# Order of the last value products, a zeroed warm-up matrix and an earlier cast of x in a gated attention and feed-forward kernel

## The chip, the cores and the metric

The kernel runs on one core of one Trainium2 chip. The metric is the device time of one execution in microseconds; several executions are timed, and their median counts. A further execution was profiled, and the profile is of that one.

## The reference, cut to what matters

The input x has 2048 rows of 512. A sigmoid gate g per row mixes two branches: a causal attention of 32 heads of 16 columns over a sliding window of 256 rows, and a feed-forward block with a SiLU gate and 1792 hidden columns.

```python
qkv = (x @ wqkv).reshape(B, S, 3, H, Dh)          # S=2048, D=512, H=32, Dh=16, W=256
scores = einsum("bhqd,bhkd->bhqk", q, k) * Dh ** -0.5
mask = (idx[:, None] - idx[None, :] >= 0) & (idx[:, None] - idx[None, :] < W)
p = softmax(where(mask, scores, -1e9))
a = einsum("bhqk,bhkd->bhqd", p, v) ... @ wo
b = (silu(x @ w_gate) * (x @ w_up)) @ w_down
g = sigmoid((x * gate_w).sum(-1))
out = g * a + (1 - g) * b
```

## The kernel before

**Tiling.** x is kept transposed, in four chunks of 512 columns (c = 0 to 3), each in four pieces of 128 rows. Precision is kept by splitting operands in two: `split` (L63) casts a high part on ScalarE (`xhi`) and subtracts it from the source on another engine (`xlo`); a projection then takes three products for each piece: high by high, low by high and high by low (`products`, L113; `whole`, L191, records at L195). The 32 heads are worked in 8 groups of 4. All order is written out by hand: each engine carries out its instructions in program order, and a tile that is needed before it is ready stops the engine that needs it.

**The start.** SyncE's queue fetches the first weights and x's first chunk piece by piece, alternating (L430 to L432), then the value weights and x's other three chunks (L433 to L436). In the meantime TensorE multiplies an identity, made by GpSimd (`make_identity`, L45), five times with itself into a tile that nobody reads (L173 to L175). Such a float32 product is two matmul instructions with a weight load each. Then come the first projections from the raw pieces (two groups, L444, 16 matmuls), value products (`vproj`) and projections of groups 0 and 1 over the later chunks, in the order of L461 to L475. `split_x(c)` (L426) is what makes a chunk of x ready: four casts on ScalarE, four subtractions on VectorE. `split_x(3)` stands at L471, behind `run(proj(1, 1, ...))` (L470), whose last act is a copy out of PSUM on ScalarE, a cast there, and a subtraction on GpSimd. The loop at L474 then projects group 0 over chunks 2 and 3.

**The main loop.** For each group and block of 128 rows (L628), scores are computed twice: `stage1` (L263) for the row maxima of the next group, `stage2` (L305) transposed for the exponentials of this one, which ScalarE writes (L307) and GpSimd masks (L309, L312). Between them TensorE works off projections and feed-forward products in two row halves (`lanes`, L215).

**The value products.** `av(g, c)` (L317) multiplies the exponentials by the values for a chunk of 512 queries. Blocks of 128 keys are named by their place m relative to the chunk's start, −2 to 3; block m touches only the queries within its window, so products near the chunk's edges are narrow. The lower 64 keys of a block go through the first 64 rows of the array into one PSUM tile, the other 64 through the last 64 rows into another tile, so two products run side by side, for each of four heads in its own 32 columns: eight products a step. L323 gives each half its own order of blocks, such that both products of a step have the same width:

| step | half 0 | half 1 | columns |
|---|---|---|---|
| 1 | m = 0 | m = 0 | 320 |
| 2 | 1 | 1 | 320 |
| 3 | 2 | −1 | 256 |
| 4 | −1 | 2 | 192 |
| 5 | −2 | 3 | 64 |
| 6 | 3 | −2 | 128 |

Chunk 0 has no blocks before it: negative m drop out there, and four steps are left, with m = 0, 1, 2, 3 in both halves. `values(t)` (L612) calls `av` three times a group: for chunks 0 and 1 together, for chunk 2 and for chunk 3. Behind each call the loop goes on with `stage1` and `stage2`. `finish` (L334) adds the two tiles, beginning with a copy on ScalarE (L342), and divides by the sums.

**The end.** Behind the main loop come the feed-forward block's last products and the output projection (L736, L83 to L85).

Of the kernel before, what the change touches and what calls it, by code (L numbers as in the profile page):

```python
# [8 lines left out]

F32 = mybir.dt.float32  # L10
F32R = mybir.dt.float32r
# [5 lines left out]
P = 128  # L17
# [16 lines left out]
def gated_mix(ctx, tc, xT, xn, w01, wqk, wv, wo, wgu, wd, gw, out):  # L34
# [4 lines left out]
    nc = tc.nc  # L39
    ctx.enter_context(tc.manual_schedule())  # L40

    const = ctx.enter_context(tc.tile_pool(name="const", bufs=1))
    dram = ctx.enter_context(tc.tile_pool(name="dram", bufs=1, space=DRAM))

    ident = const.tile([P, P], F32, name="ident")  # L45
    make_identity(nc, ident)
    vd = dram.tile([G, P, NB, VW], F32, name="vd")
    od = dram.tile([G, P, S], F32, name="od")
    mxd = dram.tile([2 * G, P, 32], F32, name="mxd")
# [13 lines left out]
    def split(hi, lo, src, hi_eng, lo_eng):  # L63
        if hi_eng is nc.scalar:
            nc.scalar.copy(hi, src)
        else:
            hi_eng.tensor_copy(hi, src)
        lo_eng.tensor_tensor(out=lo, in0=src, in1=hi.bitcast(F32), op=ALU.subtract)

    def fetch(src, raw=None):  # L70

        raw = ring.tile([P, D], F32, name="raw", bufs=1) if raw is None else raw
        nc.sync.dma_start(raw, src)
        return raw
# [14 lines left out]
    def run(gen, n=None):  # L89

        while n is None or n > 0:
            if next(gen, run) is run:
                break
            n = n and n - 1
# [5 lines left out]
    def slot(name, dtype=F32R):  # L100
        return stk.tile([P, S], dtype, name=name)

    def halves_of(t):
        n = t.shape[-1] // 2
        return [t[:, :n], t[:, n:]]
# [7 lines left out]
    def products(key, c):  # L113
        wh, wl = WT[key]
        return [(wt[:, k], xt[c][:, k]) for k in range(NK) for wt, xt in ((wh, xhi), (wh, xlo), (wl, xhi))]
# [53 lines left out]
    with ExitStack() as A:  # L169
# [1 line left out]


        warm = pp.tile([P, CH], F32, name="pa")  # L173
        for _ in range(5):
            nc.tensor.matmul(warm[:, :P], ident, ident, start=True, stop=True)  # L175

        mask = sm.tile([P, 3 * P], F32, name="mask", bufs=1)

        def kept():
            return sm.tile([P, CH], F32, name="ev", bufs=EV)  # L180
# [3 lines left out]
        def x_pair(pool=None, name="x"):  # L184
            return tuple((pool or sm).tile([P, 2 * CH], F32R, name=f"{name}{w}", bufs=1) for w in ("hi", "lo"))

        def split_qk(g, hf, cc, raw, los=nc.gpsimd):
            hi, lo = (t[:, cc * CH:(cc + 1) * CH] for t in X[g, hf])
            split(hi, lo, raw, nc.scalar, los)

        def whole(pool, name, todo, done):  # L191

            ps = pool.tile([P, CH], F32, name=name)
            for n, (w, x) in enumerate(todo):
                nc.tensor.matmul(ps, w, x, start=n == 0, stop=n == len(todo) - 1)  # L195
                if n < len(todo) - 1:
                    yield
            done(ps)
            yield
# [30 lines left out]
        def proj(g, c, pool, name, todo=None, los=nc.gpsimd):  # L230

            hf, cc = divmod(c, 2)
            if cc == 0:
                X[g, hf] = x_pair() if g == hf else x_pair(vpool, f"x{g}{hf}")

            def done(ps):
                raw = kept()
                nc.scalar.copy(raw, ps)
                split_qk(g, hf, cc, raw, los)
            return whole(pool, name, todo or products(("p", g), c), done)  # L240

        def stack(g, hf):
            for pr in range(2):
                q, k = (halves_of(t[g % 2][pr])[hf] for t in (QT, KT))
                hi, lo = (x[32 * pr:] for x in X[g, hf])
                for b, (qx, kx) in enumerate(((hi, hi), (hi, lo), (lo, hi))):
                    nc.sync.dma_start(q[b::4].bitcast(F32), qx[:32].bitcast(F32))
                    nc.sync.dma_start(k[b::4].bitcast(F32), kx[64:96].bitcast(F32))
# [68 lines left out]
        def av(g, c):  # L317


            AV[g, c] = (pp.tile([P, CH], F32, name="pb" if 4 * g + c + 1 < len(UNITS) else "pa"),  # L320
                        ps2.tile([P, CH], F32, name="ps2"))

            orders = [[4 * c + m for m in ms if 4 * c + m >= 0] for ms in ((0, 1, 2, -1, -2, 3), (0, 1, -1, 2, 3, -2))]  # L323
            for n, kbs in enumerate(zip(*orders)):
                for j in range(4):
                    for h, (o, kb) in enumerate(zip(HALVES, kbs)):
                        k0 = kb * P + 64 * h
                        q0, q1 = max(k0, c * CH), min(k0 + W + 64, c * CH + CH)
                        nc.tensor.matmul(AV[g, c][h][32 * j:32 * j + 32, q0 - c * CH:q1 - c * CH],  # L329
                                         VG[4 * g + kb // 4][o, kb % 4, 17 * j:17 * j + 32],  # L330
                                         PT[g, kb, j // 2][o, j % 2, q0 - kb * P:q1 - kb * P],
                                         start=n == 0, stop=n == len(orders[0]) - 1, skip_group_check=True)
# [61 lines left out]
        def v_products(b):  # L394
            c, o = divmod(b * P, CH)
            return [(xt[c][:, k, o:o + P], wt[:, k]) for k in range(NK)
                    for xt, wt in ((xhi, wvh), (xlo, wvh))] + \
                   [(xhi[c][:, k, o:o + P], wvl[:, k]) for k in range(NK)]
# [6 lines left out]
        def put_v(b, ps):  # L405
            t = vs[b // 2 % 2]
            nc.scalar.copy(t[:, :, b % 2, :68].rearrange("p g (j e) -> p g j e", e=17)[:, :, :, :DH],
                           ps.rearrange("p (g j e) -> p g j e", j=4, e=DH))
            if b > 3:
                send_v(b)  # L410

        def vproj(b):
            return whole(pp, "pb", v_products(b), lambda ps: put_v(b, ps))
# [8 lines left out]
        xraw = [h for w in "qk" for pr in range(2) for h in halves_of(slot(f"{w}1{pr}", F32))]  # L422
        xraw = [halves_of(h) for h in xraw]
        xraw = [[xraw[2 * c + k // 2][k % 2] for k in range(NK)] for c in range(NCH)]

        def split_x(c, ks=range(NK)):  # L426
            for k in ks:
                split(xhi[c][:, k], xlo[c][:, k], xraw[c][k], nc.scalar, nc.vector)

        for k in range(NK):  # L430
            nc.sync.dma_start(w01raw[:, k], w01[k])
            nc.sync.dma_start(xraw[0][k], xT[0, k])  # L432
        wvraw = [fetch(wv[:, k], kept()) for k in range(NK)]  # L433
        for c in range(1, NCH):
            for k in range(NK):
# [31 lines left out]
        run(proj(0, 1, pp, "pa", los=nc.vector))  # L467
        stack(0, 0)
        run(vproj(3))
        run(proj(1, 1, pp, "pa"))  # L470
        split_x(3)  # L471
        QT.append([slot(f"q1{pr}") for pr in range(2)])
        KT.append([slot(f"k1{pr}") for pr in range(2)])
        for c in range(2, NCH):  # L474
# [137 lines left out]
        def values(t):  # L612

            ag, m = divmod(t - 8, NB)
            if m == 0:
                cs, times = (0, 1), [((0, 1),) * 2 + ((0, 3), (2, 0), (2, 3)), ((0, 1), (0, 2), (1, 1), (3, 2), (4, 1))]
            else:
                cs, times = (1 + m // 4,), [((0, 1), (0, 2), (1, 1), (2, 1), (3, 1))]
            for c in cs:
                av(ag, c)  # L620
            for k, steps in enumerate(zip(*(finish(ag, c) for c in cs))):
                for todo, ts in zip(steps, times):
                    dt, hd = ts[k]
                    if (dt, hd) == (0, 1):
                        todo()
                    else:
                        FIN.setdefault((t + dt, hd), []).append(todo)
        for t in range(G * NB + 1):  # L628
# [26 lines left out]
            m = (t - 3) % NB + 3  # L655
# [188 lines left out]
```

## Time and profile before

| | us |
|---|---|
| median of 3 runs | 820.35 |
| lowest and highest | 819.96 and 820.63 |
| the profiled execution | 819.19 |
| its span in the profile | 817.2 |

In the profile PE is TensorE's matmuls, PEld its weight loads, DVE VectorE, ACT ScalarE, POOL GpSimd, SPq SyncE's queue. A row of a timeline has the start and the duration in us, the engine, the line, the operation, the tiles (out<-in), the size and the count; in square brackets stands how long the engine was idle ahead of it and who ended that. PE is busy for 810.5 us (99%), but ends of matmuls are modelled, and several overlap; DVE is busy for 63% of the span, ACT for 55%, POOL for 42%. The granted TensorE clock of the profiled execution is 1.0.

### The profile page before, as it was taken

How to read it: one execution, taken by the hardware profiler on the slowest of the kernel's cores; microseconds unless marked ns; L12 is line 12 of the kernel's file. 1: busy time of each engine (PE TensorE's matmuls, PEld its weight loads, DVE VectorE, ACT ScalarE, POOL GpSimd, SP SyncE). 2: the span in 40 equal slices, each digit the busy share in tenths (PEclk: the TensorE clock that was granted, in tenths of full speed). 3: DMA queues.
4: the chain of work that ended last, by engine and by line, in shares of the span. 5: the costliest groups of instructions: out<-in, count | busy, mean ns of one | idle time of the engine just before them, and what ended most of it. 6: DMA issues, size and time to landing. Idle time of an engine off the chain costs nothing.

```text
span 817.2 us, 21557 instructions
## 1 busy us (share of the span) xinstructions
PE 810.5 (99%) x8306; PEld 681.7 (83%) x8306; DVE 513.5 (63%) x1422; ACT 452.9 (55%) x940; POOL 343.4 (42%) x635
## 2 busy tenths in 40 slices
PE   9999999999999999999999999999999999999997
PEld 5788988888888888898888888888788888888886
DVE  5596667667668667677677678854467443443542
ACT  6422656656666666676666665666666423343341
POOL 5812546645546555654554654465610111011020
PEclk9999999999999999999999999999999999999999
DMA  8484615625634642652652565565689444463731
GB/s 295 113 262 145 182 68 165 195 76 151 184 109 118 189 147 85 175 174 70 187 179 89 161 185 165 161 217 171 216 302 322 156 139 141 159 203 103 221 89 52
DMA packets 70326, 133.27 MB, mean 163 GB/s; under 512 B 14288, under 2 KB 19024, under 8 KB 70224
## 3 DMA queue, kind: packets, MB, share of 16 engines
q1 hardware_dynamic: 65936, 116.95, 46.3%
q0 software_dynamic: 4288, 14.95, 5.1%
q8 instruction: 65, 1.06, 0.6%
q14 instruction: 37, 0.30, 0.1%
HBM read 61.08 MB, written 45.61 MB: 131 GB/s over the span
## 4 chain that ended last, share of the span: by engine, by line
PE 95%; DMA 2%; POOL 1%; SPq 1%; DVE 0%; issue 0%; ACT 0%; ACTq 0%
PE pb L215 24%; PE pa L215 24%; PE ps L85 6%; PE ps L83 6%; PE ps L84 6%; PE ps L263 6%; PE pb L329 6%; PE ps L305 5%; PE ps L329 3%; PE pb L85 2%; PE pb L83 2%; PE pb L84 2%; PE pa L736 1%; PE pb L736 1%; PE pb L195 1%; DMA k<-xT 1%
## 5 line engine op out<-in xcount | busy, mean ns | idle before, releaser
L265 DVE CUSTOM_DVE_ANT_0 ps<-ps,mask 128x384 f32<-128x384 f32 (+2 forms) x512 | 273.1, 540 | 119.0 <-PE ps L263 68.7
L307 ACT ACTIVATE pt<-ps 128x384 f32<-128x384 f32 (+2 forms) x512 | 239.4, 476 | 117.9 <-PE ps L305 57.5
L309 POOL TENSOR_SCALAR_AFFINE_SELECT pt<-pt 128x256 f32<-128x256 f32 x256 | 109.1, 426 | 222.3 <-ACT pt L307 209.3
L305 PE MATMUL ps<-q,k 64*128 64x384 f32 (+2 forms) x512 | 159.7, 326 | 0.0
L263 PE MATMUL ps<-k,q 63*128 63x384 f32 (+2 forms) x512 | 157.9, 328 | 0.0
L215 PE MATMUL pb<-xhi,wh 64*128 64x512 f32 x512 | 110.9, 393 | 0.0
L215 PE MATMUL pa<-xhi,wh 64*128 64x512 f32 x512 | 110.7, 393 | 0.0
L215 PE MATMUL pb<-xhi,wl 64*128 64x512 f32 x512 | 109.8, 392 | 0.0
L215 PE MATMUL pb<-xlo,wh 64*128 64x512 f32 x512 | 109.8, 391 | 0.0
L215 PE MATMUL pa<-xlo,wh 64*128 64x512 f32 x512 | 109.3, 391 | 0.0
L215 PE MATMUL pa<-xhi,wl 64*128 64x512 f32 x512 | 109.1, 391 | 0.0
L263 PEld LDWEIGHTS ps<-k,q 63*128 63x128 f32 x512 | 88.8, 185 | 14.2 <-issue 4.0
L312 POOL TENSOR_SCALAR_AFFINE_SELECT pt<-pt 128x256 f32<-128x256 f32 x224 | 96.9, 433 | 0.0
L305 PEld LDWEIGHTS ps<-q,k 64*128 64x128 f32 x512 | 91.4, 185 | 5.9 <-issue 0.6
L329 PE MATMUL ps<-pt,vg 64*32 64x320 f32 (+4 forms) x1408 | 75.1, 346 | 0.0
L740 DVE TENSOR_TENSOR sg<-got,sg 128x512 f32<-128x512 f32 x50 | 43.7, 874 | 48.1 <-ACT sg L739 48.1
L329 PE MATMUL pb<-pt,vg 64*32 64x320 f32 (+3 forms) x1360 | 72.3, 350 | 0.1
L265 DVE DVE_READ_ACCUMULATOR2_ANT mx<- 128x1 f32 x512 | 72.2, 141 | 0.0
L329 PEld LDWEIGHTS pb<-pt,vg 64*32 64x32 f32 x1360 | 48.8, 106 | 20.8 <-ACT pt L307 5.8
L215 PEld LDWEIGHTS pb<-xhi,wh 64*128 64x128 f32 x512 | 55.8, 185 | 8.1 <-ACT ev L529 0.2
L215 PEld LDWEIGHTS pa<-xhi,wh 64*128 64x128 f32 x512 | 55.7, 185 | 7.5 <-ACT ev L529 0.6
L215 PEld LDWEIGHTS pb<-xhi,wl 64*128 64x128 f32 x512 | 55.8, 184 | 7.1
(163 smaller groups left out, 1555.6 us busy)
## 6 DMA issues: line engine op xcount, KB each, us to landing
raws<-ev SPq DMA_DIRECT2D x100, 256.0 KB
got<-raws SPq DMA_DIRECT2D x100, 256.0 KB
od<-on POOLq DMA_DIRECT2D x32, 256.0 KB, 2.6
raw<-wgu SPq DMA_DIRECT2D x28, 256.0 KB
q<-xhi SPq DMA_DIRECT2D x56, 128.0 KB
k<-xhi SPq DMA_DIRECT2D x56, 128.0 KB
vd<-vs POOLq DMA_DIRECT2D x8, 672.0 KB, 6.0
vg<-vd SPq DMA_DIRECT2D x32, 168.0 KB
```

What stands on the lines that cost most here:

```text
L83: nc.tensor.matmul(ps, lh, rh, start=start and i == 0, stop=False)
L84: nc.tensor.matmul(ps, lh, rl, start=False, stop=False)
L85: nc.tensor.matmul(ps, ll, rh, start=False, stop=stop and i == n - 1)
L215: mm = nc.tensor.matmul(ps[me], w[r], x[r], start=not second and i == 0, stop=bool(second) and i == n - 1)
L263: nc.tensor.matmul(ps[:, :n], QT[g % 2][pr][r, q0:q0 + P], KT[g % 2][pr][r, k0:k0 + n], start=True, stop=True)
L265: mx = nc.vector.tensor_tensor_reduce(out=ps[:, :n], in0=ps[:, :n], in1=mask[:, 3 * P - n:], scale=1.0, scalar=NEG, op0=ALU.add, op1=ALU.m ...
L305: nc.tensor.matmul(ps[:, :n], KT[g % 2][pr][r, k0:k0 + P], QT[g % 2][pr][r, k0:k0 + n], start=True, stop=True)
L307: BEHIND.append(nc.scalar.activation(pt[:, j, :n], ps[:, :n], AF.Exp, scale=SCALE))
L309: nc.gpsimd.affine_select(out=pt[:, :, :P], in_=pt[:, :, :P], pattern=[[0, 2], [1, P]], compare_op=ALU.is_ge, fill=0.0, base=0, channel_mu ...
L312: nc.gpsimd.affine_select(out=pt[:, :, 2 * P:], in_=pt[:, :, 2 * P:], pattern=[[0, 2], [-1, P]], compare_op=ALU.is_ge, fill=0.0, base=-1, ...
L329: nc.tensor.matmul(AV[g, c][h][32 * j:32 * j + 32, q0 - c * CH:q1 - c * CH], VG[4 * g + kb // 4][o, kb % 4, 17 * j:17 * j + 32], PT[g, kb, ...
L740: nc.vector.tensor_tensor(out=sg, in0=gu[1], in1=sg, op=ALU.mult)
```

## The change

Three places are edited.

- In `av` the last two steps of the six change places: the products of 128 columns come fifth, those of 64 columns sixth, in both halves. For chunk 0 the lists stay as they are.
- The warm-up matrix is a tile of zeros, written by one VectorE memset at the head of that engine's work; GpSimd makes no identity any more. The warm-up has six products instead of five. The first piece of x is fetched by ScalarE's queue; all other loads stay on SyncE's.
- `split_x(3)` stands ahead of `run(proj(1, 1, ...))` instead of behind it.

```diff
-from concourse.masks import make_identity
...
-    ident = const.tile([P, P], F32, name="ident")
-    make_identity(nc, ident)
+    zero = const.tile([P, P], F32, name="zero")
+    nc.vector.memset(zero, 0.0)
...
-        for _ in range(5):
-            nc.tensor.matmul(warm[:, :P], ident, ident, start=True, stop=True)
+        for _ in range(6):
+            nc.tensor.matmul(warm[:, :P], zero, zero, start=True, stop=True)
...
-            orders = [[4 * c + m for m in ms if 4 * c + m >= 0] for ms in ((0, 1, 2, -1, -2, 3), (0, 1, -1, 2, 3, -2))]
+            orders = [[4 * c + m for m in ms if 4 * c + m >= 0] for ms in ((0, 1, 2, -1, 3, -2), (0, 1, -1, 2, -2, 3))]
...
             nc.sync.dma_start(w01raw[:, k], w01[k])
-            nc.sync.dma_start(xraw[0][k], xT[0, k])
+            (nc.sync if k else nc.scalar).dma_start(xraw[0][k], xT[0, k])
...
         run(vproj(3))
+        split_x(3)
         run(proj(1, 1, pp, "pa"))
-        split_x(3)
```

## The prediction

> **What bounds the kernel now.** I read the page first: the chain that ended last is matmul time on TensorE for nearly the whole span, so a nanosecond taken off TensorE's own sequence is a nanosecond off the end, and DVE, ACT and POOL matter only where TensorE waits for one of them.
>
> ```profile
> span 817.2 us, 21557 instructions
> ...
> PE 95%; DMA 2%; POOL 1%; SPq 1%; DVE 0%; issue 0%; ACT 0%; ACTq 0%
> ```
>
> Second I read the waits of the weight loads (PEld) over the whole span: who was waited for, us in total, times, longest.
>
> ```profile
> PEld ps L263 <- issue: 4.0, 20, 0.2
> ...
> PEld ps L305 <- issue: 0.6, 3, 0.2
> ...
> PEld pa L736 <- issue: 0.2, 1, 0.2
> ```
>
> These are 20 + 3 + 1 = 24 waits of 0.2 us, 4.8 us in all, and nothing is waited for. Twenty-four is also the number of places where the value products (L329) end: 8 groups with three runs each (chunks 0 and 1 together, then 2, then 3). So third I read the timeline of one such place, first TensorE's matmuls (start us, us).
>
> ```profile
> 128.85 0.32 PE L329 MATMUL pb<-pt,vg 64*32 64x192 f32 x1
> ...
> 129.02 0.22 PE L329 MATMUL pb<-pt,vg 64*32 64x64 f32 x1
> ...
> 129.13 0.27 PE L329 MATMUL pb<-pt,vg 64*32 64x128 f32 x1
> ...
> 129.44 0.27 PE L329 MATMUL ps<-pt,vg 64*32 64x128 f32 x1
> 129.64 0.44 PE L263 MATMUL ps<-k,q 63*128 63x384 f32 x1
> ```
>
> Eight products (four heads by two row halves) run side by side, each in two passes. The eight 64-column products have both passes started and streamed between 129.02 and 129.13: 0.056 us a pass. Then come the 128-column ones. The first starts at once, at 129.13; the last starts its second pass only at 129.44. Streaming alone would put that at 129.13 + 0.11 + 0.05 = 129.29. Why it is late stands in the weight loads of the same stretch:
>
> ```profile
> 129.07 0.16 PEld L329 LDWEIGHTS pb<-pt,vg 64*32 64x32 f32 x2
> 129.21 0.10 PEld L329 LDWEIGHTS ps<-pt,vg 64*32 64x32 f32 x1
> ...
> 129.34 0.11 PEld L329 LDWEIGHTS ps<-pt,vg 64*32 64x32 f32 x1
> 129.64 0.18 PEld L263 LDWEIGHTS ps<-k,q 63*128 63x128 f32 x1 [0.20 <-issue]
> ```
>
> The load for the second 128-column product goes out only at 129.21, and the rest are strung out until 129.34, when the last product begins its first pass (the load for a product's second pass goes out as its first begins). From there to the next line's load is 129.64 − 129.34 = 0.30 us: two passes of 0.107 (129.34 to 129.44 is one) and 0.09 to empty the array, behind which the 128-wide load of L263 goes.
>
> What holds the load at 129.21? It is 0.04 behind the recorded end (128.85 + 0.32 = 129.17) of the second pass of a 192-column product, which stands 17 products earlier in the program. I read this as a window of some 16 products: the next is let in when an old one is done. [...]
>
> **The swap (L323).** In chunks 1 to 3 the last two of the six steps change places: 128 columns, then 64. Nothing is added or removed, and chunk 0 keeps its order, since steps at negative blocks drop out. The 192-column products that open the window stay where they are, so the loads of the last step's products go out when they do now, and the last product begins its first pass at about 129.34 again, now with 64 columns. The 128-column step ahead of it starts at 129.02 and has streamed its two passes by 129.02 + 2 × 0.107 + 0.05 = 129.28, so it is not later than that. What is left behind the last load is two passes of 0.056 in place of two of 0.107: 0.10 us saved, with the 0.09 to empty the array unchanged. Times 24: 2.4 us. Bounds: if the next load went a fixed 0.20 behind the start of the last pass, whatever its length, only one pass is shortened, 0.05 × 24 = 1.2 us. If nothing held the loads, the last first pass would start 0.05 sooner (129.28 + 0.01), 0.15 × 24 = 3.6 us. I take 2.4, because 0.20 splits well into a pass of 0.107 and a remainder, and because the loads have a visible cause that does not move. What follows the place on TensorE is again bound by TensorE, by the chain. ACT's copy of the sums is released 0.10 sooner, and nothing waits for it there. The data of the newest block is first needed in the fifth step in both orders, so no new wait.
>
> [...]
>
> **x's last quarter cast sooner (L471 to before L470).** Fourth I looked at the one other place where TensorE waits visibly:
>
> ```profile
> 28.70 0.59 ACT L238 COPY ev<-pa 128x512 f32<-128x512 f32 x1 [2.12 <-PE pa L195]
> ...
> 29.84 2.18 ACT L65 CAST xhi<-k 128x512 fp32r<-128x512 f32 x4
> ...
> 30.49 1.98 DVE L68 TENSOR_TENSOR xlo<-k,xhi 128x512 fp32r<-128x512 f32 x2 [3.68 <-DMA k<-xlo]
> ...
> 30.99 0.39 PE L195 MATMUL pa<-xhi,wl 128*128 128x512 f32 x1
> ...
> 31.22 0.39 PE L195 MATMUL pa<-xhi,wh 128*128 128x512 f32 x1
> ...
> 31.91 0.19 PEld L195 LDWEIGHTS pa<-xlo,wh 128*128 128x128 f32 x1 [0.73 <-DVE xlo L68]
> 31.92 0.50 PE L195 MATMUL pa<-xlo,wh 128*128 128x512 f32 x1 [0.31 <-DVE xlo L68]
> ```
>
> The projection over x's last quarter has its second matmul at 31.92 instead of 31.22 + 0.23 = 31.45: 0.47 us lost, and a little at the restart (0.50 against 0.39 for that matmul), so 0.6. It waits for DVE's first subtraction, that for ACT's first cast at 29.84 (DVE's wait is named as a DMA, but the cast ends as it ends), and ACT stands idle for 2.12 us before 28.70, in program order behind a copy that waits for TensorE. The moved step is four casts and four subtractions, no DMA. In that gap, from 28.70 − 2.12 = 26.58, the casts take 2.18 and end at 28.76. The copy they now stand ahead of slips by 0.06, and with it the cast and the POOL subtraction behind it; they feed a stack that is sent long after. DVE was idle for 3.68 us in the same stretch and has the first subtraction done near 28, over 3 us ahead of need. All 0.6 goes, if x's last quarter has landed by 26.58. A bound for that: the load issued behind it in the same queue had landed at
>
> ```profile
> 15.15 5.14 DMA raw<-wgu
> ```
>
> 15.15 + 5.14 = 20.29. What is late next is TensorE itself. Bounds: 0.47 and 0.6; I take 0.6.
>
> **The head.** The warm-up reads a zeroed matrix, made by one DVE memset, in place of POOL's memset and select, and has six products (12 matmuls) instead of five; x's first piece goes out from ACT's queue at once rather than second on SP's.
>
> ```profile
> 1.26 0.42 SPq L432 DMA_DIRECT2D q<-xT  x1
> 1.32 1.22 POOL L388 MEMSET vs<- 128x1344 f32 x1
> 1.43 2.21 PEld L175 LDWEIGHTS pa<-ident 128*128 128x128 f32 x10 [1.43 <-POOL ident masks.py:199]
> ...
> 4.17 7.51 PE L195 MATMUL pa<-q,vs 128*128 128x512 f32 x16 [0.23 <-DMA q<-xT]
> ```
>
> SP's 14 later loads go out 0.45 sooner (0.42 of issuing and a gap), x's first piece likewise. But the warm-up now holds TensorE for 2.21 / 10 × 12 = 2.65 us, 0.44 more, from perhaps 0.1 sooner (the memset is short and first on DVE): to about 4.0 or 4.1, where the products of x begin at 4.17 today. So they begin 0.1 sooner. No price on ACT: its table load waits for one DMA issue and has over a microsecond to spare before x is there. POOL only loses work. How much of an earlier start survives ACT's casts behind it no row shows; bounds are one issue spacing either way, 0.45 sooner or 0.45 later (two queues sharing the engines may bring the first weights or a later piece later). I take 0.1, nearest to where the longer warm-up ends.
>
> **Sum.** 2.4 + 0.6 + 0.1 = 3.1 us. The profiled execution took 819.19 us (span 817.2), 1.2 below the median of 820.35. The sum makes it 816.1, and the median 820.35 − 3.1 = 817.25; I say 817.3.
>
> **Rivals.** All keep 0.6 + 0.1 unless said.
> - *Fixed delay*: the next line's load follows the last pass's start by 0.20 whatever its length. 1.2 + 0.7 = 1.9: 818.5. For it: all 24 waits are 0.2. Against it: all 24 end on the same width, so they can't tell, and 0.09 after a pass is a more natural emptying.
> [...]
> - *The zeroed matrix does not wake the clock.* Of the 16 matmuls from 4.17 on one took 1077 ns, the others 592 (min, median, max):
>
> ```profile
> L195 PE MATMUL pa<-q,vs x16: 592/592/1077, 4.2 to 11.1; 128*128 128x512 f32 x16
> ```
>
> I read this as full speed from about 5.1, 3.7 us after the warm-up began. With a warm-up that counts for nothing it would come 3.7 after 4.1, 2.7 later than now, and half-speed work over that time costs 1.3: 820.35 − 3.1 + 1.3 = 818.6. Against it: the identity is itself all zeros but for one element a row, and it seems to have been enough.
> - *Slower*: the hold in the loads is not set 17 products back but by the step's own first product, 129.21 − 129.13 = 0.08 behind it, and a 64-column pass can't cover the 0.107 of its own load. Then after the swap: first product at 129.24, last load 129.24 + 0.08 + 0.09 (the loads' spread now) = 129.41, first pass 0.03 later, second pass 0.107 later (129.55), and the next load 0.20 behind: 129.75 against 129.64, 0.11 × 24 = 2.6 lost, less 0.7: 822.2. It decides as soon as the hold exceeds what the shorter passes give, 0.10. Against it: the 64-column loads now come ahead of their own step's first product.
>
> **How the numbers follow.** The forecast has 0.62 (with it the better end, 816.0 or so), the fixed delay 0.15, no gain from the swap 0.11, the clock 0.07, slower 0.05. The range holds the forecast with its bounds (2.4 to 3.6, and 0.45 at the head: down to 820.35 − 3.6 − 0.6 − 0.45 = 815.7), the fixed delay, the clock and no gain from the swap: 815.7 to 819.7. About 0.2%, 1.6 us, is what a measurement of this kernel can tell from no change: up to 818.7 counts as faster. That is the forecast but for its worst end, two thirds of the fixed delay, half of the clock: 0.74. Same is the rest without the slower case: 0.21.
>
> **What would show it.** In the profile after: the 24 waits named issue still there, but the last L329 matmul 64 columns wide, and from the first 192-column pass at such a place to the next load of L263 0.10 us less, with the loads of the last step starting where they start now. PEld's wait on xlo gone, ACT's idle 2.12 filled by the four casts, the copy of L238 at 28.7 to 28.8 (less what the head gives). The products of x starting at 4.0 to 4.1. Wrong would be: last loads moved by more than 0.05, the next load again 0.20 behind the last pass's start, a second matmul of x at over 0.43 us spacing for long (clock), or the first wait for a DVE or ACT row in the run of matmuls from 34 us on.

## The result and the profile after

| | before | after |
|---|---|---|
| median (6 runs each) | 820.49 | 816.29 |
| lowest to highest | 819.8 to 821.34 | 815.41 to 816.6 |
| the profiled execution | 819.19 | 815.41 |
| its span | 817.2 | 813.7 |

After to before 0.9947, 95% interval 0.9934 to 0.996: 4.2 us less (3.3 to 5.4 by the interval's ends), where 3.1 were forecast. The two profiled spans differ by 3.5. Lines of the kernel after are one lower, since an import is gone: its L328 is L329 before.

The weight loads' waits of after, whole span, as shown of before:

```profile
PEld pb L194 <- issue: 0.8, 3, 0.3
...
PEld ps L262 <- issue: 0.2, 1, 0.2
```

Of the 24 waits of 0.2 us at the ends of the value products one is left in the list, which shows none of 0.15 us or less; the others have become shorter (0.09 at most places). The wait on x's low part is gone from the list. The same place as before, TensorE's matmuls first:

```profile
127.49 0.32 PE L328 MATMUL pb<-pt,vg 64*32 64x192 f32 x1
...
127.66 0.27 PE L328 MATMUL pb<-pt,vg 64*32 64x128 f32 x1
...
127.77 0.27 PE L328 MATMUL pb<-pt,vg 64*32 64x128 f32 x1
...
127.87 0.22 PE L328 MATMUL pb<-pt,vg 64*32 64x64 f32 x1
...
128.03 0.22 PE L328 MATMUL ps<-pt,vg 64*32 64x64 f32 x1
128.17 0.44 PE L262 MATMUL ps<-k,q 63*128 63x384 f32 x1
```

and its weight loads:

```profile
127.77 0.11 PEld L328 LDWEIGHTS pb<-pt,vg 64*32 64x32 f32 x1
127.85 0.10 PEld L328 LDWEIGHTS ps<-pt,vg 64*32 64x32 f32 x1
...
127.97 0.11 PEld L328 LDWEIGHTS ps<-pt,vg 64*32 64x32 f32 x1
128.17 0.18 PEld L262 LDWEIGHTS ps<-k,q 63*128 63x128 f32 x1
```

The 128-column step now starts both its passes on the beat (127.66, 127.77). The hold in the loads is still there: the second load of the last step goes out at 127.85, 0.36 behind the point at which the second passes of the 192-column step begin (127.49), and before it was 129.21 − 128.85 = 0.36 as well. The last load is at 0.48 behind that point (127.97), before at 0.49. From it to the next line's load are 0.20 us now (128.17) and 0.30 before. That is the gain of 0.107, and it stands at 17 of the 24 places in the trace (0.105 to 0.108).

At six places, those where a new group's first scores follow, it is smaller: 0.05 at five, 0.02 at one. There the last value product is followed by this:

```profile
L262 PEldq EVENT_SEMAPHORE  x3: 51/51/51, 144.1 to 144.3; - x3
L262 PEld LDWEIGHTS ps<-k,q x1: 183/183/183, 144.4 to 144.4; 63*128 63x128 f32 x1
```

Three instructions in TensorE's own queue that only wait for semaphores start 0.11 us apart, and the load behind them is what now ends last. At one place the gain is 0.24: before, its last step was held up for 0.13 us, by what no row shows (POOL's last mask ahead of it had ended 2.9 us earlier). In sum 2.3 us over the 24 places.

x's last quarter, timelines of after (ACT, DVE and PE rows):

```profile
25.82 2.18 ACT L64 CAST xhi<-k 128x512 fp32r<-128x512 f32 x4
...
26.48 2.50 DVE L67 TENSOR_TENSOR xlo<-k,xhi 128x512 fp32r<-128x512 f32 x4 [0.48 <-ACT xhi L64]
...
28.06 0.59 ACT L237 COPY ev<-pa 128x512 f32<-128x512 f32 x1
...
30.58 0.39 PE L194 MATMUL pa<-xhi,wh 128*128 128x512 f32 x1
30.81 0.39 PE L194 MATMUL pa<-xlo,wh 128*128 128x512 f32 x1
```

The second product follows the first by 0.23 where it was 0.70. And the start:

```profile
1.12 2.93 PE L174 MATMUL pa<-zero 128*128 128x128 f32 x12 [1.12 <-DVE zero L45]
4.22 7.27 PE L194 MATMUL pa<-q,vs 128*128 128x512 f32 x16 [0.17 <-DMA q<-xT]
```

The first product of x is not earlier (4.22, before 4.17), but the 16 matmuls take 7.27 instead of 7.51, and the first projection over x's second chunk began at 19.70 instead of 20.34.

### The profile page after: what moved, and what is told of

Same layout as the page of the kernel before. It is cut to its first block, busy times and chain, and to the rows that moved or that the text cites. A ratio compares the mean times of both kernels' runs of the same rounds, so it can differ in the third digit from the quotient of the medians.

```text
span 813.7 us, 21560 instructions
## 1 busy us (share of the span) xinstructions
PE 807.6 (99%) x8308; PEld 697.7 (86%) x8308; DVE 512.2 (63%) x1423; ACT 453.6 (56%) x940; POOL 343.1 (42%) x633
## 4 chain that ended last, share of the span: by engine, by line
PE 99%; DMA 0%; ACT 0%; DVE 0%; issue 0%; ACTq 0%
PE pb L214 24%; PE pa L214 24%; PE ps L83 6%; PE ps L82 6%; PE ps L84 6%; PE ps L262 6%; PE pb L328 6%; PE ps L304 5%; PE ps L328 3%; PE pa L194 2%; PE pb L194 2%; PE pb L83 2%; PE pb L82 2%; PE pb L84 2%; PE pa L735 1%; PE pb L735 1%
## 5 line engine op out<-in xcount | busy, mean ns | idle before, releaser
L214 PE MATMUL pb<-xhi,wh 64*128 64x512 f32 x512 | 113.7, 393 | 0.0
L214 PE MATMUL pa<-xhi,wh 64*128 64x512 f32 x512 | 113.3, 393 | 0.0
L214 PE MATMUL pb<-xhi,wl 64*128 64x512 f32 x512 | 112.6, 392 | 0.0
L214 PE MATMUL pb<-xlo,wh 64*128 64x512 f32 x512 | 112.5, 391 | 0.0
L214 PE MATMUL pa<-xlo,wh 64*128 64x512 f32 x512 | 112.3, 391 | 0.0
L214 PE MATMUL pa<-xhi,wl 64*128 64x512 f32 x512 | 112.2, 391 | 0.0
L328 PE MATMUL ps<-pt,vg 64*32 64x320 f32 (+4 forms) x1408 | 72.4, 345 | 0.0
L328 PE MATMUL pb<-pt,vg 64*32 64x320 f32 (+3 forms) x1360 | 69.7, 349 | 0.1
L328 PEld LDWEIGHTS pb<-pt,vg 64*32 64x32 f32 x1360 | 48.7, 106 | 20.8 <-ACT pt L306 6.6
L214 PEld LDWEIGHTS pb<-xhi,wh 64*128 64x128 f32 x512 | 58.8, 185 | 5.4
L214 PEld LDWEIGHTS pb<-xhi,wl 64*128 64x128 f32 x512 | 58.6, 184 | 4.9
L214 PEld LDWEIGHTS pa<-xhi,wl 64*128 64x128 f32 x512 | 58.4, 184 | 5.0
```

Of the source, the lines that this page charges most:

```text
L214: mm = nc.tensor.matmul(ps[me], w[r], x[r], start=not second and i == 0, stop=bool(second) and i == n - 1)
```

## The experiments

The theory after the result: three gains that add up, 2.3 us at the 24 places, 0.6 at x's last quarter, and at the head more than the 0.1 forecast. The rival for the head: luck of one profiled execution.

**Each part alone.** Three kernels, each the kernel before with one part of the diff shown above.

Swap alone:

> The kernel before with the swap alone. If the swap's share is what the traces of before and after show at the 24 places (107 ns at most of them), it gives 2.2 to 2.4 us: about 818.2 where before has 820.5, span 2.2 to 2.4 shorter, and 0.14 us from the last 64-column pass's start to the next load. If the fixed delay of 0.20 behind the last pass held, 1.2 us; if the gain after came from elsewhere (a wait on POOL gone by luck of timing), under 1 us.

Measured: 817.46 against 819.89 of before, measured beside it, ratio 0.997 (0.9959 to 0.9982): 2.4 us less. At 18 of its 24 places there is the same 0.14 from the start of the last 64-column pass to the next load as after; at the six group starts it is 0.20, where the three waiting instructions stand. The fixed delay is refused. In its profiled execution the 24 places give only 1.9 us, since two of them were held up for 0.14 and 0.33 us by something else.

Cast alone:

> The kernel before with x's last quarter cast sooner alone: 0.6 us less, the wait of the weight loads on xlo gone, the first lanes product 0.6 sooner against the first projection of group 1 over chunk 1. Rival: the stall moves to the next product and 0 to 0.2 is left.

Measured: 819.08 against 819.89; 0.9988 (0.998 to 0.9997), about 0.8 to 1.0 us. The trace is sharper: from the first projection over x's second chunk to the first product in two row halves (L215) it took 34.16 − 20.47 = 13.69 us, before 34.67 − 20.34 = 14.33, after 13.69. So 0.64.

Head alone:

> The kernel before with the head alone (zeroed matrix, six warm-up products, x's first piece by ScalarE's queue). Theory: the head is paced by the landing of the value weights that ScalarE casts, which come 0.6 sooner as all loads go out sooner: 0.6 us less, first projection of group 1 over chunk 1 near 25.1 instead of 25.8. Rival: the after trace was a lucky draw of landings and clock, and the head alone gives 0.1 or nothing in the median, with a landing of the third value-weight piece near 11.2 as before.

Measured: 818.91 against 819.89; 0.9988 (0.9979 to 0.9997), 1.0 us. Yet its profiled execution was no faster than before up to 20 us (20.54 against 20.34). The landings I had named were no sooner: ScalarE cast the value weights from 10.07 on, where before cast them from 9.77. The gain was there in the median; the cause that I had named was not.

**The halves of the head.** The queue alone,

```diff
-            nc.sync.dma_start(xraw[0][k], xT[0, k])
+            (nc.sync if k else nc.scalar).dma_start(xraw[0][k], xT[0, k])
```

> The kernel before with x's first piece by ScalarE's queue alone (identity, five warm-up products). The head as a whole gave 1.0 us. If that is the loads' doing (x's fourth piece landed at 7.8 to 8.1 instead of 8.9 to 9.3 in the profiles so far), this gives most of it, 0.6 to 1.0. If it is the warm-up's doing (no gap ahead of the first product of x, so that full clock comes at the first chance), this gives 0 to 0.2, or a loss of some tenths, because the first weights now share the way and land at 4.2 instead of 2.9.

gave 820.02 against 819.7: 1.0004 (0.9995 to 1.0013), nothing or a loss. The zeroed matrix with six products alone,

```diff
-    make_identity(nc, ident)
+    nc.vector.memset(zero, 0.0)
...
-        for _ in range(5):
+        for _ in range(6):
```

> The kernel before with the zeroed matrix and six warm-up products alone, all loads by SyncE's queue. Warm-up theory: 0.6 to 1.0 us in the median, with the full clock granted below 6.5 us from the start; loads theory: 0 to 0.2. Should a zeroed matrix not wake the clock, it would be slower by over 1 us, with the full clock 3 us later.

gave 819.62 against 819.7: 0.9998 (0.9989 to 1.0007), nothing. So neither half carries the 1.0 us, and both single theories fall. But the profile of the queue alone has this:

```profile
1.43 2.50 PE L175 MATMUL pa<-ident 128*128 128x128 f32 x10 [1.43 <-POOL ident masks.py:199]
4.55 9.52 PE L195 MATMUL pa<-q,vs 128*128 128x512 f32 x16 [0.62 <-DMA q<-xT]
```

There is a gap of 0.62 us ahead of the products of x, and the 16 matmuls then take 9.52 us, 2 us more. What TensorE waits for in the gap is x's first piece. It was issued 0.45 us sooner, beside the first weights, and yet landed later:

```profile
4.53 0.62 ACT L65 CAST xhi<-q 128x512 fp32r<-128x512 f32 x1 [2.01 <-DMA q<-xT]
```

By the landings that the trace holds, x's first piece came at 4.51 here and at 4.03 in the kernel before, the first weights at 4.34 and 2.93. The expectations above and below put the gap down to the first weights; they did land later, but 0.17 us ahead of x's piece. The profile of six zeroed products alone has no slow stretch, but another stall:

```profile
4.22 2.02 PE L194 MATMUL pa<-q,vs 128*128 128x512 f32 x4 [0.17 <-DMA q<-xT]
6.67 5.39 PE L194 MATMUL pa<-q,vs 128*128 128x512 f32 x12 [0.44 <-DMA q<-xT]
```

With all loads on SyncE's queue x's second piece came too late. With the queue it was cast at 5.13 to 5.49 in the traces with six products, without it at 5.77 to 6.56. From this the next theory: the halves need each other; the sixth product covers the later landing, and the queue brings x's later pieces.

> The head alone on the kernel before, once more: it gave 1.0 us (0.3 to 1.7), while its two halves gave -0.3 and 0.1. Theory: the halves belong together, since the queue makes the first weights land at 4.2 to 4.4 instead of 2.9 and only the sixth product covers that gap: again 0.6 to 1.2, with the full clock below 7 us. Rival: the 1.0 was the luck of a few executions, whose starts differ by up to 2 us with the clock and the landings: 0 to 0.4.

Measured for the head alone once more: 818.71 against 819.79; 0.9989 (0.9979 to 0.9998), 1.1 us. The 1.0 was no luck.

The spans on record divide this gain in two. Each measured time is longer than the span of the same execution, and the difference is 1.66 to 1.78 us in every run of every kernel that has both the zeroed matrix and x's first piece on ScalarE's queue, whatever the number of products, and 1.99 to 2.13 in every run of the others, each half alone included. That is 0.33 us, and no row shows what it is. The span itself is 0.7 us shorter with the head alone (817.2 against 817.9, and 817.0 against 817.7, medians).

> The head alone with five zeroed products instead of six. They end near 3.6, and the first product of x comes at 4.2 to 4.4, a gap of 0.6 to 0.8. Theory of the gap: in part of the executions the full clock comes a window later, at 8 to 9.5 us, as in the two profiles so far with such a gap, and the median is 0.5 to 1.5 us above that of six products. Rival, the gap is of no matter: the same as six within 0.3.

```diff
-        for _ in range(6):
+        for _ in range(5):
```

Measured with five zeroed products: 820.12 against 819.79; 1.0006 (0.9997 to 1.0015), so 1.4 us above six, all of it in the span (818.4 against 817.0). Its profile:

```profile
1.12 2.50 PE L174 MATMUL pa<-zero 128*128 128x128 f32 x10 [1.12 <-DVE zero L45]
4.29 10.11 PE L194 MATMUL pa<-q,vs 128*128 128x512 f32 x16 [0.67 <-DMA q<-xT]
```

and of the head with six:

```profile
1.12 2.93 PE L174 MATMUL pa<-zero 128*128 128x128 f32 x12 [1.12 <-DVE zero L45]
4.48 8.04 PE L194 MATMUL pa<-q,vs 128*128 128x512 f32 x16 [0.43 <-DMA q<-xT]
```

Gap 0.67 against 0.43, stretch 10.11 against 8.04. Over all 14 profiles of this case, in the order of the third column, with the 16 matmuls at full speed being worth about 7.0 us (15 x 0.43 + 0.59):

| start | idle ahead of x's products, us | full speed from, us | the 16 matmuls, us |
|---|---|---|---|
| five products, x by SyncE | 0.23, 0.25, 0.14, 0.70 | 5.00, 6.39, 7.47, 8.84 | 7.51, 8.20, 8.79, 9.20 |
| five products, x by ScalarE | 0.62, 0.67 | 9.39, 10.31 | 9.52, 10.11 |
| six products, x by ScalarE | 0.17, 0.30, 0.43, 0.15, 0.23, 0.41 | 4.54, 4.68, 6.33, 6.35, 6.47, 6.91 | 7.27, 7.28, 8.04, 8.18, 8.21, 8.33 |
| six products, x by SyncE | 0.17 | 4.35 | in two parts |
| none (below) | no warm-up | 8.31 | 9.11 |

The third column is from the record of the granted clock that each kept trace holds: it is where its first entry, full speed, begins. At that point the starts of the matmuls go from 0.85 us apart to 0.43. (The 1.00 that the profile's rows give from the start of the span on, and the 1.0 given above for the kernel before, only mean that the record has no entry ahead of that one.) Over all 13 stretches in one part, the later the full speed, the longer the stretch. The full-speed entries last 805.54, 808.96 or 812.37 us, in steps of 3.41, so I divide the time ahead of full speed into periods of 3.41 us too. In all 14 traces TensorE idled for at most 0.43 us in the period that ends where full speed begins, and for at least 0.62 in the one before it. From this I estimate that a gap of 0.62 cost a whole period and one of 0.43 did not; where between them a limit lies is not shown. For the same six products with x's first piece by ScalarE's queue full speed began at 4.54 to 6.91. The three starts with a gap over 0.6 (9.20 to 10.11 us for the 16 matmuls) were no better than the one without warm-up (9.11).

One more period of 3.41 us with starts 0.85 us apart instead of 0.43 would be an estimated 1.7 us (four matmuls fewer, at 0.43); the three with a gap over 0.6 took 9.6 on average, the nine others in one stretch behind a warm-up 8.0.

And without warm-up:

> The kernel after without warm-up products (nothing of the result hangs on them). If they wake the clock, full clock comes about 3.6 us or more behind the first product of x, near 8 to 9 us instead of 4.3 to 6.9, and the start is 1 to 2 us slower than after: 817.2 to 818.2. If a zeroed matrix counts for nothing, nothing changes: 816.2.

```diff
-        for _ in range(6):
+        for _ in range(0):
```

Measured: 817.59, 0.9972 (0.9962 to 0.9981) of before, where after has 0.9947 and 0.9959 in its two measurements. So the six zeroed products are worth about 1 to 2 us. A matrix of zeros does wake the clock: full speed came at 4.35 to 6.91 with six zeroed products and at 8.31 without.

**Where the 64-column step stands.** If the loads of whatever follows a step of 0.11 us are strung out, as those of the 128-column step were before (129.21 to 129.34), the step could also stand first, with no such step ahead of it.

```diff
-            orders = ... ((0, 1, 2, -1, 3, -2), (0, 1, -1, 2, -2, 3))
+            orders = ... ((-2, 0, 1, 2, -1, 3) if c else (0, 1, 2, 3), (3, 0, 1, -1, 2, -2) if c else (0, 1, 2, 3))
```

> The kernel after, but in chunks 1 to 3 the 64-column step stands first of six, ahead of the 320-column ones. If a window of some 16 products is what strings out the loads, the short step costs nothing at the head of a run, where the next loads are let in by then; no load is late, and a place takes 2.30 us from its first load to the next line's load against 2.37 now: 1.7 us less than after, 814.6. If each place has to wait for the newest block's exponentials and its mask on POOL, which the first step now needs, the wait stands ahead of the first load and eats 0.1 to 1 us a place: 816 to 840. If a 64-column step costs its loads wherever it stands, same as before the swap, 818.5.

Measured: 815.78, 0.9949 of before (0.9935 to 0.9963), no clear difference from after. Its trace says why. In the runs of chunks 2 and 3 all 16 places but two took 2.32 us from the first product to the next line's load, 0.05 less than after's 2.37 and 0.11 less than its 2.43 at a group's start. But in the runs of chunks 0 and 1 the step now follows chunk 0's last, in the middle, and seven of the eight took 4.21 as before, 0.106 more than after: the hold is back where the 320-column products follow the short step. Rows of the matmuls at one such seam:

```profile
239.71 0.45 PE L328 MATMUL pb<-pt,vg 64*32 64x320 f32 x1
239.73 0.45 PE L328 MATMUL ps<-pt,vg 64*32 64x320 f32 x1
239.74 0.45 PE L328 MATMUL pb<-pt,vg 64*32 64x320 f32 x1
```

The 320-column products behind the 64-column ones start 0.015 to 0.02 apart, where 0.007 is the beat. Of the wait for the newest block's mask, which I had feared, there is little: two of the 24 places took 0.1 us longer. A third took 0.18 longer, but in its last step, where the kernel before was held up too.

So the step first in chunks 2 and 3, last in chunk 1:

> The kernel after, with the 64-column step first in chunks 2 and 3 alone; chunk 1, which follows chunk 0 in one run, keeps the order of after. In the run with the step first in all chunks, places of chunk 2 took 52 ns less than after and those of chunk 3 up to 111 ns less, while those of chunks 0 and 1 took 106 ns more. Leaving those out should give 8 x 0.052 + 8 x 0.1 = 1.2 us less than after in the same call. If the gain is taken back by waits elsewhere (ScalarE's copy of the sums, POOL's mask for the newest block), 0 to 0.5.

Measured: 815.6 against 819.7; 0.995 (0.9937 to 0.9962). The kernel after beside it:

> The kernel after once more, beside the others on one chip: 4.2 us less than before, as first measured, and as the three parts alone sum to (2.4 + 0.8 to 1.0 + 1.0).

816.0, 0.9959 (0.9946 to 0.9971). The mixed order is 0.4 lower by the medians, and the intervals overlap. In the traces the part from the first scores to the end is 1.2 us shorter, as expected (776.3 against 777.5; 777.2 in the first profile of after); its start at the head differs from execution to execution by as much. Its median is the lowest of the kernels run, but by the ratio to before it does not stand out from after's 0.9947 and 0.9959.

The mixed order with the old head:

> The kernel before with the cast moved and the mixed order of the value products (64 columns first in chunks 2 and 3, last in chunk 1), but its own head. With the new head the same took 815.6. Head worth 1.0: 816.6. Head worth nothing: 815.6 to 815.8. From before: swap 2.4 + 1.2 for the mixed order + 0.8 to 1.0 for the cast, 4.5.

816.35 against 819.79; 0.9958 (0.9945 to 0.9971). With the new head it was 0.995: the head is worth 0.7 here, though the two were not measured side by side.

## Why the prediction was right, and where it was not

- **The whole**: 817.3 forecast, 816.29 measured, inside the range. The direction held; 4.2 us came where 3.1 were forecast, and nearly all of the difference is the head's.
- **The swap**: forecast 2.4, alone 2.4, in the trace 2.3. The loads of the last step did stay where they were, both of the last product's passes got shorter (0.056 instead of 0.107), and the 0.09 behind the last pass, which the prediction puts down to the emptying of the array, was the same for both lengths. The rival of the fixed delay is refused by the 0.14 from the last pass's start to the next load (0.20 before), "slower" by the 0.107 gained. No run shows the case of no gain from the swap, to which the forecast gives 0.11 and which sets the upper end of its range: the swap alone gained 2.4 us. That the cause of the hold is a window of some 16 products is the author's estimate: it is argued from the hold's place 17 products back, from its staying at 0.36 (127.49 to 127.85) when the step behind the opener changed, and from its return in the middle of the long runs; no run shows how long such a window is. Not foreseen: at the six group starts only 0.02 to 0.05 came, as three semaphore waits in TensorE's queue were next. That lost some 0.4 us over the six, and 0.13 came at one place by luck, so the sum is nearer to the forecast than its parts.
- **The cast**: forecast 0.6, 0.64 in the trace. ScalarE's copy did not slip (28.06, which is 2.92 behind the projection's first product at 25.14; before, 28.70 and 25.78), DVE was done in time (28.98, for a product at 30.81).
- **The head** is the term that was mis-sized: "I take 0.1", bounds 0.45 either way; measured 1.0 and 1.1. I priced the head by when x's first product begins, taking it that x's first piece would come 0.45 sooner. It did not: it landed at 4.18 (4.03 before), and its first product began at 4.22 (4.17 before; 4.0 to 4.1 forecast). What the runs showed in its place is two gains. Some 0.7 us lie in the span, and hang on what I had named as side conditions: how long TensorE idles between warm-up and work, which went with when full speed came (4.35 to 7.47 with at most 0.43 us of idling, 8.84 to 10.31 with 0.62 to 0.70), and when x's later pieces land. How the 0.7 divides between these two was not measured. The other 0.33 us lie outside the span, come only when both halves are there, and their cause stays open. I had set the longer warm-up down as a cost of 0.44 us of holding TensorE; it is what the gain in the span hangs on.
- **The clock rival** was answered: zeroes count (full speed at 4.35 to 6.91 with six zeroed products, 8.31 without). The prediction read full speed from about 5.1 in the profile of before, and the trace's record has 5.00; but that was one draw of several, the other three with the same head having 6.39 to 8.84.

That both halves of the head are needed is shown. That it is the clock which makes the difference between five and six products is read from one profile of each kind and fits all 14; the executions that were only timed have no such record.

## What to carry to other kernels

Where narrow matmuls run side by side, look at the weight loads behind them: here a step of 0.11 us let the loads of whatever followed it fall behind, 0.107 us at 17 of 24 places, so try it where nothing of its kind follows, at the end of a run or at its head. Look at the gap between a warm-up and the first real product: here 0.62 to 0.70 us ahead of that product undid the warm-up (full speed at 8.84 to 10.31, and at 8.31 without one), and a change that made x's first piece land at 4.51 instead of 4.03 opened such a gap. Parts that do nothing alone can be worth something together, so test the whole beside its halves.

## What the runs showed of the hardware

- A load of another tile shape went out 0.09 us behind the streaming of the last value product, for a last pass of 0.107 as well as of 0.056 (0.20 and 0.14 from that pass's start).
- Instructions that only wait for semaphores follow each other by 0.11 us in TensorE's queue though each takes 0.05, and three of them were enough to cut a gain of 0.107 us to 0.05 at five places and to 0.02 at a sixth.
- With x's first piece on a second queue, issued at the same time as the first weights, these landed at 3.95 to 4.34 us (nine traces) instead of 2.79 to 3.02 (five). The piece itself, issued 0.45 us sooner, landed no sooner: at 4.16 to 4.51, against 3.94 to 4.08 in four of the five and 4.49 in the fifth.
- Full speed of TensorE began at 4.35 to 10.31 us, in each of 14 traces at the end of a period of 3.41 us with at most 0.43 us of idling, and multiplying zeroes counted as work (4.35 to 6.91 with six zeroed products, 8.31 without).
- The start of the kernel is in part a matter of luck: up to the first projection over x's second chunk profiles of the same head differ by 1.1 us (19.70 to 20.84, six profiles) and 1.5 (20.34 to 21.85, four).
